# Rank matmuls behind a chunk's row products, and the first expert chosen after 12 chunks instead of 18

## The chip, the cores and the metric

The kernel runs on one core of a Trainium2 chip. Time is device microseconds (us) of one execution, and the figure for a kernel is the median of several runs. The engines are named as the profile names them: PE (TensorE), DVE (VectorE), ACT (ScalarE), POOL (GpSimd) and SP (SyncE, which here only issues DMAs). Each engine works through its own list of instructions in order and waits on semaphores for the others.

## What is computed

Three layers follow each other: a linear attention with a decaying state, a mixture of 8 experts in which each token goes to one expert, and a dense layer.

```
state = alpha[t] * state + k[t] (x) v[t];  y[t] = q[t] @ state       # 4 x 8 heads, 768 steps, 48 wide
x = y as 3072 rows of 384
e = argmax(x @ w_gate);  gate = softmax(x @ w_gate)[e];  eom = sigmoid(x @ w_output_gate)[e]
x = gate * eom * (relu(x @ w1[e]) @ w2[e])                           # 8 experts, 384 -> 1024 -> 384
out = relu(x @ w_in)**2 @ w_out                                      # 384 -> 2048 -> 384
```

## The kernel before

**Chunks.** Attention runs over 24 chunks of 128 tokens (six for each of four batch entries), all heads together, in the loop `for i in range(NCH - 2)`, with two chunks written out behind it. The program is in manual order: each engine executes what the Python code emits, in that order. Iteration i does several chunks' work at once: `scores(i + 1)` (key-query products, then the masked copies `m`, one by DVE and one by ACT and POOL's affine select), `scaled(i + 2)` (transposes of k and q into `tr`, scaled to `kh` and `qh` on DVE), `rows(i - 1)` and `logits(i - 1)` (chunk i - 1 turned to rows of tokens, the product `fx`, and the gate's logits), `decay(i + 3)` (transposes of alpha and two scans on DVE), `khat(i + 1)`, `outputs(i)` (the product `y`), `check(i)` and `update(i + 1)` (the product `u` and the state `st`). `load` refills a slot of k, q, alpha or v from SP's queue as soon as it is read; there are three or four slots of each.

**Routing.** Chunks are routed in groups of 6, 6, 6, 3, 1, 1 and 1. When a group's logits are there, `route` or `route_one` emits some small DVE steps, two at each `pulse()` between other work. `ranks` counts on PE where each token stands among its expert's tokens (`rk`), `place` and `placed` make of that a row index `idx` and a gate `g`, and `move` scales three tokens' chunks at a time (ACT for even, DVE for odd chunks) and scatters them with an indirect DMA on POOL to the table `xs`, which has a region for each expert. Before, `scores(i + 1)` emitted the rank matmuls ahead of its masks and `place` behind them: for the first two groups an iteration late (the set `waited`), for the later ones at once. Their result lay in the buffer of `y`, for three chunks in that of `ku`.

**The early start.** The experts' stage does not wait for all tokens. `pick` takes the expert with most tokens so far, `choose(0)` brings its number into an SP register (SP's queue waits for that), and `fetch` loads the raw float32 weights of six units of its hidden layer, two DMAs of 192 KB for each unit. `parts` splits a unit into two float32r parts: ACT copies, then DVE or POOL subtracts. `gather_early` reads the expert's first 256 rows from `xs`, `turn_early` transposes them (`tx`), and `up1(0)` is the first expert matmul (`ha`). Before, `pick` and the loads stood at the end of iteration 19 (NCH - 5) and took the counts of 18 chunks; of the first four units POOL subtracted two (iterations 20 and 22) and DVE two (both in iteration 21).

If the chosen expert has under 256 tokens (`few`), a general path runs behind the program; it is not taken for these inputs.

## Time and profile before

| | us |
|---|---|
| three runs | 831.48, 834.2, 836.35 |
| median | 834.2 |
| profiled execution, its own time | 830.97 |
| its span, first to last instruction | 829.2 |
| mean granted TensorE clock | 0.989 |

Of the span PE is busy 96%, DVE 60%, ACT 46% and POOL 28%; but the attention stage, up to about 169 us, has other limits than the rest: there DVE is busy 8 or 9 tenths of nearly every slice, and later 3 to 7. Times in the rows below are counted from the start of the span. The busy time of PE is modelled from the starts of its instructions, so a wait can hide in it; a wait stands in square brackets behind the row of the instruction that ended it.

### The profile page before, as it was taken

How to read it: one execution, taken by the hardware profiler on the slowest of the kernel's cores; microseconds unless marked ns; L12 is line 12 of the kernel's file. 1: busy time of each engine (PE TensorE's matmuls, PEld its weight loads, DVE VectorE, ACT ScalarE, POOL GpSimd, SP SyncE). 2: the span in 40 equal slices, each digit the busy share in tenths (PEclk: the TensorE clock that was granted, in tenths of full speed). 3: DMA queues.
4: the chain of work that ended last, by engine and by line, in shares of the span. 5: the costliest groups of instructions: out<-in, count | busy, mean ns of one | idle time of the engine just before them, and what ended most of it. 6: DMA issues, size and time to landing. Idle time of an engine off the chain costs nothing.

```text
span 829.2 us, 14100 instructions
## 1 busy us (share of the span) xinstructions
PE 796.7 (96%) x5215; PEld 731.1 (88%) x5215; DVE 498.4 (60%) x969; ACT 381.3 (46%) x734; POOL 228.6 (28%) x275
## 2 busy tenths in 40 slices
PE   7999999899999999999997999999999999999995
PEld 5899998798899999999986997999999999999995
DVE  8889999857355645876687787443333333333331
ACT  3677777554454555555444344332333333333221
POOL 3002341628456766777200000210002002002002
PEclk9999999899999999999998999999999999999998
DMA  9999994544554655674112110000000000000001
GB/s 135 179 210 180 209 175 99 185 132 157 156 161 128 182 149 152 167 181 127 39 58 76 58 58 21 39 13 27 0 1 39 1 1 38 1 1 39 1 0 42
DMA packets 153860, 74.98 MB, mean 90 GB/s; under 512 B 105406, under 2 KB 149430, under 8 KB 153782
## 3 DMA queue, kind: packets, MB, share of 16 engines
q1 hardware_dynamic: 149878, 64.52, 35.1%
q0 software_dynamic: 3904, 9.47, 3.1%
q8 instruction: 43, 0.70, 0.4%
q14 instruction: 35, 0.29, 0.1%
HBM read 61.76 MB, written 12.20 MB: 89 GB/s over the span
## 4 chain that ended last, share of the span: by engine, by line
PE 44%; issue 32%; DVE 14%; ACT 4%; POOL 3%; DMA 1%; SPq 1%; ACTq 0%; POOLq 0%; DVEq 0%
PE ha L1334 5%; PE ha L1336 5%; PE acc L1335 5%; PE acc L1334 5%; PE ha L1335 5%; PE acc L1336 5%; PE tr L268 3%; PE fx L425 2%; PE y L404 2%; POOL out_dram L129 2%; PE sc L337 2%; DVE r L929 2%; PE y L400 2%; ACT hh L933 2%; DVE bits L1346 1%
## 5 line engine op out<-in xcount | busy, mean ns | idle before, releaser
L1334 PE MATMUL ha<-xh,w 128*128 128x512 f32 (+7 forms) x456 | 173.9, 381 | 4.4 <-ACT xh L913 4.4
L1335 PE MATMUL ha<-xl,w 128*128 128x512 f32 (+7 forms) x456 | 172.3, 378 | 1.0 <-DVE xl L914 1.0
L1336 PE MATMUL ha<-xh,w 128*128 128x512 f32 (+7 forms) x456 | 172.5, 378 | 0.0
L929 DVE SCALAR_TENSOR_TENSOR r<-ha,r 128x512 f32<-128x512 f32 x96 | 66.3, 690 | 139.9 <-ACT r L928 137.6
L171 POOL TENSOR_TENSOR w<-raw,w 128x768 fp32r<-128x768 f32 x60 | 112.4, 1873 | 76.9 <-ACT w L170 73.9
L1334 PE MATMUL acc<-w,hh 128*128 128x384 f32 x384 | 130.6, 340 | 2.4 <-ACT half L946 1.8
L129 POOL DMA_INDIRECT out_dram<-o,ids x24 | 24.5, 1021 | 392.4 <-ACT o L954 359.8
L1336 PE MATMUL acc<-w,hl 128*128 128x384 f32 x384 | 130.6, 340 | 0.1
L1335 PE MATMUL acc<-w,hh 128*128 128x384 f32 x384 | 130.4, 340 | 0.0
L928 ACT ACTIVATE r<-ha 128x512 f32<-128x512 f32 x96 | 57.2, 596 | 144.4 <-PE ha L1336 144.3
L934 DVE TENSOR_TENSOR hl<-r,hh 128x512 fp32r<-128x512 f32 x96 | 66.6, 693 | 66.3 <-ACT hh L933 48.5
L1334 PEld LDWEIGHTS ha<-xh,w 128*128 128x128 f32 x456 | 85.9, 188 | 14.4 <-ACT xh L913 5.2
L1336 PEld LDWEIGHTS ha<-xh,w 128*128 128x128 f32 x456 | 85.8, 188 | 14.0
L933 ACT CAST hh<-r 128x512 fp32r<-128x512 f32 x96 | 59.5, 620 | 83.8 <-DVE r L929 82.6
L1335 PEld LDWEIGHTS ha<-xl,w 128*128 128x128 f32 x456 | 85.9, 188 | 11.6 <-DVE xl L914 1.9
L1334 PEld LDWEIGHTS acc<-w,hh 128*128 128x128 f32 x384 | 72.7, 189 | 7.3 <-ACT half L946 2.2
L170 ACT CAST w<-raw 128x768 fp32r<-128x768 f32 x64 | 53.5, 836 | 55.5 <-PE acc L1336 39.4
L1335 PEld LDWEIGHTS acc<-w,hh 128*128 128x128 f32 x384 | 72.7, 189 | 3.9
L1336 PEld LDWEIGHTS acc<-w,hl 128*128 128x128 f32 x384 | 72.7, 189 | 0.4 <-DVE hl L934 0.4
L703 DVE SCALAR_TENSOR_TENSOR hl<-ha,hh 128x448 fp32r<-128x448 f32 (+7 forms) x58 | 33.6, 580 | 54.8 <-ACT hh L700 52.3
L1334 PE MATMUL acc<-hh,w 128*128 128x448 f32 (+7 forms) x174 | 61.4, 353 | 0.0
L1335 PE MATMUL acc<-hl,w 128*128 128x448 f32 (+7 forms) x174 | 60.8, 350 | 0.1
(215 smaller groups left out, 1317.9 us busy)
## 6 DMA issues: line engine op xcount, KB each, us to landing
raw<-in_moe_w_dram SPq DMA_DIRECT2D x128, 192.0 KB
bits<-in_moe_w_in_dram SPq DMA_DIRECT2D x16, 384.0 KB
bits<-in_moe_w_out_dram SPq DMA_DIRECT2D x16, 384.0 KB
nat_al<-in_alpha_dram SPq DMA_DIRECT2D x24, 192.0 KB
nat_k<-in_k_dram SPq DMA_DIRECT2D x24, 192.0 KB
nat_q<-in_q_dram SPq DMA_DIRECT2D x24, 192.0 KB
nat_v<-in_v_dram SPq DMA_DIRECT2D x24, 192.0 KB
gx<-xs SPq DMA_DIRECT2D x22, 192.0 KB
```

What stands on the lines that cost most here:

```text
L129: ins = nc.gpsimd.indirect_dma_start(out=dst[:, :], out_offset=bass.IndirectOffsetOnAxis(ap=ix, axis=0), in_=src, in_offset=None)
L170: nc.scalar.copy(w[:, 0::2, :], raw)
L171: engine.tensor_tensor(out=w[:, 1::2, :], in0=raw, in1=w[:, 0::2, :].bitcast(F32), op=ALU.subtract)
L268: nc.tensor.transpose(ps[:, pr, :], src[:, pr, :], ident)
L703: nc.vector.scalar_tensor_tensor(out=hl, in0=ps, scalar=0.0, in1=hh.bitcast(F32), op0=ALU.max, op1=ALU.subtract)
L928: nc.scalar.activation(r, ps, AF.Relu)
L929: nc.vector.scalar_tensor_tensor(out=r, in0=ps, scalar=0.0, in1=r, op0=ALU.max, op1=ALU.mult)
L933: nc.scalar.copy(hh, r)
L934: nc.vector.tensor_tensor(out=hl, in0=r, in1=hh.bitcast(F32), op=ALU.subtract)
L1334: nc.tensor.matmul(ps, st[0], mv[0], start=start, stop=False)
L1335: nc.tensor.matmul(ps, st[0], mv[1], start=False, stop=False)
L1336: nc.tensor.matmul(ps, st[1], mv[0], start=False, stop=stop)
```

## The change

The rank matmuls and `place` leave `scores` and go to a new function `settle`, which is called behind `outputs(i)`, for each group as soon as it is routed. For a group of six their result lies in the buffer of `fx`. `pick` takes the counts of two groups (12 chunks) and stands in iteration 14, with `choose(0)` and the twelve loads; whether the chosen expert has 256 tokens after 18 chunks is asked by the new function `enough`, in iteration 20. `parts` of units 0 to 3 stand at the end of iterations 16, 17, 19 and 21, all with POOL's subtraction. Behind the loop, the last group's scaling and scatters (`send_group`) go from before `turn_early` to behind `outputs(23)`, and `turn_early` goes ahead of the logits of chunk 21.

```diff
@@ scores(i)
-            held = [(gi, ranks(gi)) for gi in list(routing) if gi in waited or gi >= PICK - 1]
-            waited.update(routing)
...
-            for gi, ps in held:
-                place(gi, ps)
+        def settle():
+            for gi in list(routing):
+                place(gi, ranks(gi))
@@ psum(n)
-                t = p_1.tile([P, BLK], F32, tag="ku" if n == 3 else "y", name="rk")
+                t = p_1.tile([P, BLK], F32, tag="fx" if n == GROUPS[0] else "y", name="rk")
@@ pick and enough
-            key = keys(PICK, ei8, "key0")
+            key = keys(PICK - 1, ei8, "key0")
-            nc.vector.tensor_scalar(few, mx, float(E * EARLY), None, op0=ALU.is_lt)
+        def enough():
+            n = keys(PICK, pre, "key1")
+            nc.vector.tensor_reduce(out=few, in_=n, axis=AX.X, op=ALU.max)
+            nc.vector.tensor_scalar(few, few, float((1 << 16) + E * EARLY), None, op0=ALU.is_lt)
@@ the loop
+        ready = [gstart[PICK - 1] + x for x in (4, 5, 7, 9)]
         for i in range(NCH - 2):
-            if i == NCH - 3:
-                parts(1, nc.vector)
...
-                parts(2, nc.vector)
...
             outputs(i)
+            settle()
...
-            if i == NCH - 5:
+            if i == gstart[PICK - 1] + 2:
                 pick()
                 for n in range(NRA + 2):
                     fetch(n)
             if i == NCH - 4:
+                enough()
                 gather_early()
-                parts(0)
+            if i in ready:
+                parts(ready.index(i))
@@ behind the loop, chunk 23
-        parts(3)
...
         i = NCH - 1
+        steps = [turn_early(kk) for kk in range(NK)]
+        settle()
         logits(i - 2)
         finish()
-        steps = [turn_early(kk) for kk in range(NK)]
         outputs(i)
+        send_group()
```

Three places where the order changes. On DVE, from the last product of chunk 23's `qh` to the one-hot of the group of three (iteration 21), before:

```order
L318 TENSOR_TENSOR qh<-tr,sp 128x512
L171 TENSOR_TENSOR w<-raw,w 128x2x384
L442 TENSOR_REDUCE lg<-fx 128x16
L171 TENSOR_TENSOR w<-raw,w 128x2x384
L463 TENSOR_REDUCE mx<-lg 128x3
L466 TENSOR_TENSOR df<-lg,mx 128x24
L471 SCALAR_TENSOR_TENSOR cand<-df,em_94 128x24
```

and after:

```order
L318 TENSOR_TENSOR qh<-tr,sp 128x512
L442 TENSOR_REDUCE lg<-fx 128x16
L463 TENSOR_REDUCE mx<-lg 128x3
L466 TENSOR_TENSOR df<-lg,mx 128x24
L471 SCALAR_TENSOR_TENSOR cand<-df,em_94 128x24
```

The two weight subtractions `w` have left DVE's list. On POOL, from iteration 19 to the split in iteration 21 of the changed kernel (`xs` is the scatter of a chunk, `m` the mask of a chunk's second half of heads; five more pairs of memset and scatter stand where the dots are):

```order
L171 TENSOR_TENSOR w<-raw,w 128x2x384
L347 AFFINE_SELECT m<-m 128x512
L128 MEMSET apart 128x1
L129 DMA xs<-xn,idx 24576x384
...
L347 AFFINE_SELECT m<-m 128x512
L171 TENSOR_TENSOR w<-raw,w 128x2x384
```

Before, the six scatters of chunks 12 to 17 stood three and three, with a mask between them; now all six stand in a row ahead of the mask of chunk 22, and a split stands ahead of them and another behind that mask. On SP, at the end of iteration 14 of the changed kernel, the choice and the first of twelve weight loads:

```order
L260 DMA nat_al_156<-in_alpha_dram 128x8x48
L260 DMA nat_v_174<-in_v_dram 128x8x48
L148 TENSOR_LOAD first
L148 ISA x2
L159 ISA
L159 DMA raw<-in_moe_w_dram 128x3x128
L160 ISA
L160 DMA raw<-in_moe_w_dram 128x384
```

Behind the twelfth stand the loads of k, q, alpha and v for iterations 15 and on, 16 in all; before, the choice stood behind the loads of iteration 19, which are the last of them.

## Rows read from the trace of the kernel before

**Rows 1.** Busy time by stretch: us, then busy us (instructions) of each engine, granted clock, DMA
```profile
107.60:113.84 6.24, 6.24 (x84) 5.94 (x81) 5.47 (x12) 4.84 (x12) 1.66 (x3) 1.00 0.91 147
...
145.54:153.27 7.73, 6.61 (x80) 5.84 (x76) 6.57 (x10) 5.90 (x11) 6.72 (x9) 1.00 0.95 305
153.27:157.31 4.04, 1.17 (x20) 1.07 (x17) 3.83 (x13) 0.77 (x3) 1.55 (x2) 0.80 0.52 190
```
**Rows 2.** The same view in stretches of 2 us, around the half clock
```profile
154.00:156.00 2.00, 0.43 (x8) 0.34 (x7) 1.93 (x6) 0.03 (x1) 0.82 (x1) 0.93 0.62 232
156.00:158.00 2.00, 0.69 (x7) 0.68 (x7) 1.86 (x9) 0.92 (x3) 0.00 (x0) 0.50 0.04 16
...
160.00:162.00 2.00, 2.00 (x14) 1.77 (x15) 1.04 (x1) 0.92 (x2) 1.10 (x1) 0.50 0.00 0
162.00:164.00 2.00, 2.00 (x23) 1.83 (x20) 1.96 (x7) 0.58 (x1) 1.07 (x3) 0.86 0.00 0
```
**Rows 3.** PE in order of time: start, us, line, instruction [idle before, what ended it]
```profile
126.66 0.66 PE L268 MATMUL tr<-ident,nat_k 128*128 128x128 f32 x4
...
157.31 0.18 PE L503 MATMUL rk<-onehot,tri 128*128 128x24 bf16 x1 [2.88 <-DVE st L385]
...
162.82 0.87 PE L692 MATMUL tx<-ident,gx 128*128 128x128 f32 x6
163.53 1.06 PE L400 MATMUL y<-qh,both 128*128 128x128 f32 x8
...
169.29 0.39 PE L1334 MATMUL ha<-early,w 128*128 128x256 f32 x1
```
**Rows 4.** DVE in order of time, same columns, iterations 19 to 21
```profile
140.94 0.16 DVE L653 SCALAR_TENSOR_TENSOR key<-cps,ei 128x8 f32<-128x8 f32 x1
...
144.02 1.22 DVE L294 TENSOR_TENSOR_SCAN sp<-al,ends 128x512 f32<-128x512 f32 x1
...
149.98 0.68 DVE L318 TENSOR_TENSOR qh<-tr,sp 128x512 f32<-128x512 f32 x1
151.78 2.54 DVE L171 TENSOR_TENSOR w<-raw,w 128x768 fp32r<-128x768 f32 x1 [1.12 <-issue]
...
154.38 1.25 DVE L171 TENSOR_TENSOR w<-raw,w 128x768 fp32r<-128x768 f32 x1
...
156.40 0.18 DVE L479 SCALAR_TENSOR_TENSOR onehot<-ei,em 128x24 bf16<-128x24 f32 x1
```
**Rows 5.** ACT in order of time, iteration 20: the scaling of a chunk
```profile
144.40 0.66 ACT L574 ACTIVATE xn<-xn,g 128x384 f32<-128x384 f32 x1
```
**Rows 6.** POOL in order of time: scatters of group 2 and the last of all
```profile
148.15 0.97 POOL L129 DMA_INDIRECT xs<-xn,idx  x1 [0.59 <-DVE xn L572]
...
150.69 0.96 POOL L129 DMA_INDIRECT xs<-xn,idx  x1 [0.19 <-issue]
...
174.19 0.96 POOL L129 DMA_INDIRECT xs<-xn,idx  x1 [0.19 <-ACT early L700]
```
**Rows 7.** SP in order of time: first weight load, early gather, last gather of the first expert
```profile
142.71 0.40 SPq L159 DMA_DIRECT2D raw<-in_moe_w_dram  x1
...
157.24 0.89 SPq L684 DMA_DIRECT2D gx<-xs  x2
176.93 0.86 SPq L892 DMA_DIRECT2D rest<-xs  x2
```
**Rows 8.** PE in order of time: a wait in the first chunks
```profile
25.27 0.66 PE L268 MATMUL tr<-ident,nat_al 128*128 128x128 f32 x4 [1.63 <-DMA nat_al<-in_alpha_dram]
```
**Rows 9.** Busy time by stretch, around that wait
```profile
24.00:26.00 2.00, 0.73 (x7) 0.73 (x8) 0.85 (x3) 0.60 (x2) 0.63 (x1) 1.00 1.50 166
```
**Rows 10.** Groups by line, 200 to 400 us: POOL's splits, busy us, mean ns | idle before
```profile
L171 POOL TENSOR_TENSOR w<-raw,w 128x768 fp32r<-128x768 f32 x55 | 103.2, 1877 | 64.9 <-ACT w L170 61.9 <-DMA gx<-xs 1.0 <-DMA raw<-in_moe_w_dram 0.9
```
**Rows 11.** The same view of DVE, 200 to 400 us: a step beside the splits
```profile
L1346 DVE SCALAR_TENSOR_TENSOR bits<-sq,bits 128x384 f32<-128x384 f32 x16 | 21.6, 1350 | 16.0 <-ACT sq L1344 14.2 <-DMA gx<-xs 1.9
```
**Rows 12.** The same view, 400 to 600 us: the same DVE step without POOL's splits
```profile
L1346 DVE SCALAR_TENSOR_TENSOR bits<-sq,bits 128x384 f32<-128x384 f32 x16 | 8.9, 556 | 0.5
```

More of the change, by code (lines that the diff above doesn't have):

```diff
@@ L446, in logits @@
                 agenda.append((route if GROUPS[gi] > 1 else route_one)(gi))
-        routing, waited = {}, set()
+        routing = {}
         def route(gi):
@@ L638, in place_one, with send_group @@
                                            scalar=float(E * NT), in1=ix, op0=ALU.add, op1=ALU.add)
+        def send_group():
+            for i, g in moving:
+                x = xn.pop(i)
+                nc.vector.tensor_scalar(x, x, g, None, op0=ALU.mult)
+                scatter("xs", xs, idx[:, i:i + 1], x)
         def send(i):
@@ L802, in moe_block_kernel @@
         rows(i - 1)
-        parts(3)
         finish()
         outputs(i)
-        for i, g in moving:
-            x = xn.pop(i)
-            nc.vector.tensor_scalar(x, x, g, None, op0=ALU.mult)
-            scatter("xs", xs, idx[:, i:i + 1], x)
         i = NCH - 1
+        steps = [turn_early(kk) for kk in range(NK)]
+        settle()
         logits(i - 2)
         finish()
-        steps = [turn_early(kk) for kk in range(NK)]
         outputs(i)
+        send_group()
         one = group[i - 2][0]
```

## The prediction

> **What bounds the kernel now.** I read the busy times by stretch first, to find where attention stops running at its normal pace, then the engines in order of time inside that place, and last the DMA issues. A normal chunk takes 6.24 us, and PE is busy in all of it [rows 1]: in the middle of attention PE sets the pace, and work that DVE, ACT or POOL do beside it is free while they keep up. That ends near iteration 21. The stretch from 145.54 is 7.73 us long with 6.61 us of PE work, and the next is 4.04 us long with 1.17 us of PE work [rows 1]. The reader is to see who held it: DVE's `qh` ends at 150.66, then DVE waits 1.12 us and subtracts a weight for 2.54 us, takes the logits, and subtracts another for 1.25 us; only then come the one-hot at 156.40 and the state, for which the rank matmuls waited 2.88 us [rows 3, 4]. PE had so little to do that its granted clock fell to half: 0.93 on average in 154 to 156, 0.50 from 156 on, 0.86 in 162 to 164 [rows 2]. From the averages the half clock lasted 0.28 + 6 + 0.56 = 6.8 us. The first expert matmul starts at 169.29 [rows 3]. From there PE is the bound almost to the end (busy 96% of the span), so what that start gains should reach the end of the kernel; it is the quantity that I forecast.
>
> **DVE's halves go.** Two weight subtractions leave DVE, and with them the wait for ACT's copies: from the end of `qh` to the one-hot were 156.40 - 150.66 = 5.74 us, of which 1.12 + 2.54 + 1.25 = 4.91 us [rows 4] fall away. On its own this puts the one-hot at 151.5. The rank matmuls now stand ahead of `u` and the scores of chunk 23 (1.17 us busy [rows 1], and I estimate 0.6 for `u`). The products from 157.31 to 162.82 took 5.51 us, nearly all at half clock; at full clock I take 2.9. So chunk 22's products end at about 151.5 + 0.2 + 0.6 + 1.2 + 2.9 = 156.4, instead of 162.82: over 6 us earlier.
>
> **But the early gather then ends last.** The transposes `tx` stand next on PE, and they need the 256 gathered rows. Before, these were long there. The gather waits for the scatters of chunks 12 to 17, and the change makes those later: their group is placed behind `outputs(19)`, not ahead of it, so its reciprocal comes right behind the scan of iteration 20, and all six scatters follow in a row. The scan started at 144.02 [rows 4]. Three things move it. The choice leaves iteration 19: seven small steps of about 0.16 us, -1.05 us. In iteration 14 these steps come between PE's count and the next `fx`, in whose buffer the count lies: I take +0.5 us, bounds 0 and 1.05. POOL's splits delay DVE: +0.25 us, below. I take the scan at 143.7. It lasts 1.22, the reciprocal 0.2, ACT's scaling 0.66 [rows 5]: first scatter at 145.8. Three scatters started from 148.15 to 150.69, one each 1.27 us [rows 6]. So the sixth starts at 152.15 and ends on POOL at 153.1; before it ended at 151.65. What gains here is the rest of the way. The old gather was issued at 157.24, 5.6 us behind the last scatter, because twelve weight loads had been sent from 142.71 on [rows 7]; the last gather of this expert, with no such load in the queue, followed its scatter's end (174.19 + 0.96) by 1.78 us [rows 6, 7]. That gives an issue at 154.9. The old one moved nothing any more from 160.00 on [rows 2], so it needed at most 2.76 us: rows there at 157.7. With `tx` (163.53 - 162.82 = 0.71 us [rows 3]) chunk 23's `y` starts at 158.4 instead of 163.53. **Gain: 5.1 us.** PE waits about 1.3 us ahead of `tx`; a wait of 1.63 us left the clock at 1.00 [rows 8, 9], one of 2.88 us did not [rows 2, 3]. So I expect no half clock. From that `y` to the first expert matmul were 5.76 us [rows 3], in a chain of PE, ACT and DVE steps that stays. The three scalings of the last group move behind `outputs(23)`, but the DVE steps for which they wait are done while PE runs that product. I leave it at 5.76.
>
> **What must stay hidden.** Four ACT copies move to iterations 16, 17, 19 and 21; in a normal chunk ACT is busy 4.84 of 6.24 us [rows 1], so each has room, and two scalings leave iterations 16 and 17. If the cover fails, the copy (the same work as before, then in iterations 20 to 22) delays the scan behind it by its own length, under 1 us. On POOL a split of 1.88 us [rows 10] fits into a chunk where POOL is busy 1.66 [rows 1], behind the mask of one chunk and ahead of the next. What it does to DVE is the open cost: the step L1346 takes 1.350 us where splits run and 0.556 where none does [rows 11, 12], +0.8 us for a step that is hit. Three splits come before the scan of iteration 20: bounds 0 and 2.4 us. I take 0.25, since DVE has 0.8 us to spare in a normal chunk (5.47 of 6.24 [rows 1]) and only the third split meets a full one.
> The rule that speaks against the change is in the Trainium skill, SBUF — State Buffer, section "Who interferes with whom": a VectorE instruction with two SBUF inputs and a GpSimd instruction that reads SBUF share a port, and who comes second waits for the whole instruction of the first. The trace agrees in kind (2.54 us for a subtraction beside POOL's, 1.25 without), but its mean price is half a split or less. By the rule each split could stop a scan for its full 1.88 us, 5.6 us for three, and nothing would be left of the gain.
>
> The moved choice holds SP's queue in iteration 14 until DVE has it, by estimate near 111 us (the next chunk's PE work starts at 107.60 [rows 1], DVE ends its share some 2 us behind PE, and the seven steps take 1.05), and then twelve loads of 192 KB; before, the first went out 0.1 us behind the choice's last steps and the data of all twelve had come by about 156, 13 us later (0.62 DMA share in 154 to 156, 0.04 after [rows 2, 7]). So the loads of chunk 20's k, q, alpha and v wait until 111 + 13 = 124; k is needed at 126.66 [rows 3]. Its own load needs 1 to 2 us more. It fits with about 1 us left; bounds of this cost: 0, and 3 us if k comes at 129.
>
> For the default inputs the counts, taken from the reference, give the same first expert after 12 chunks (215 tokens) and after 18 (319, above 256), so neither the general path nor another order of experts comes in.
>
> **Rivals.** (1) The gather comes 1.2 us later or more, by splits, copies or slower scatters, and PE waits long enough to fall to half clock as before. Then `tx`, `y` and two `fx`, some 4.5 us at full clock, take up to 3.4 us more (6.8 at half [rows 2]): gain 5.1 - 1.2 - 3.4 = 0.5, **833.7**. For it: six scatters in a row; against it: a wait of 1.63 us did no harm. (2) The splits stop DVE's scans for their full length: three times 1.88 us [rows 10], 5.6 us, in place of my 0.25: gain 5.1 + 0.25 - 5.6 = -0.2, **834.4**; against it stands +0.8 in rows 11 and 12. (3) Slower than before: the loads of k, q and alpha for chunk 20 come behind the weights and PE stands still in iteration 18. With k late by d us the loss is d, and from about 2.7 us on also 3.4 us for the half clock. At d = 5, k at 131.7, the gain turns into 5.1 - 5 - 3.4 = -3.3, **837.5**; it decides from d = 1.7 if the clock falls with it. For it: only about 1 us of slack; against it: the queue is idle at 111, and has three scatters beside it, not six as at 142. (4) The chain behind `y` also shortens, because its ACT and DVE steps are no longer late behind POOL and half-clock products: of its 5.76 us perhaps 2.5, gain 7.6, **826.6**.
>
> **How the numbers follow.** Forecast 0.52, rival 1 0.18, rival 2 0.10, rival 3 0.09, rival 4 0.11. The sum stands against the profiled execution: 830.97 - 5.1 = 825.9. The median of the three runs is 834.2, 3.2 above, so I forecast 829.1. The forecast's own spread is about 2.5 us on either side (scan 143.0 to 145.5, loads 0 to 1 late). The range from 824.5 to 835.0 leaves out rival 3, and the ends of rival 4. A difference of 0.5%, 4.2 us, is about what a measurement of this kernel can tell from no change: faster by more, 0.53 (most of the forecast, rival 4); within, 0.38; slower by more, 0.09.
>
> **What would show it.** In the changed profile: no DVE weight subtraction before the first expert matmul; that matmul at about 164.2; PE's longest wait ahead of `tx`, released by the gather, under 2 us, and the granted clock at 1.00 from 140 to 170; the six scatters from about 146 to 153 and the gather's issue near 155. Wrong would be: PE waiting for nat_k or nat_al near 127 (rival 3), DVE scans of 2 us and more beside splits (rival 2), a clock of 0.5 near 158 (rival 1). If the start of the experts comes earlier as forecast and the time does not, a later stage has taken the gain back.

## The result

The changed kernel takes 839.6 us (median of 8 runs, 835.3 to 841.04) against 832.5 for the kernel before on the same chip: ratio 1.0072, 95% interval 1.0048 to 1.0096. It is 7 us slower, by 0.7%; I had forecast 829.1 and a gain of 5.1. The profiled execution took 839.43 us, its span is 837.6 (before 829.2), the mean granted clock 0.985 (before 0.989).

To see where the time went, I followed one marker through both traces: the start of each chunk's scores on PE, then the first expert matmul, then the issue of the rest gather (of the first expert's other rows) on SP. The other columns are runs described below.

```
us from the span's start      before   after  e1_clear  e2_enough  e3_rank_fx  e4_send  e5_all  e12_late_question
scores of chunk 12             82.43   83.42     83.12      82.00       82.50    82.26   82.71     81.95
scores of chunk 13             89.49   93.67     90.56      88.91       91.86    93.03   89.13     88.19
scores of chunk 20            130.96  137.60    133.64     132.01      136.58   139.13  132.20    130.39
scores of chunk 22            145.54  151.47    147.50     145.76      150.43   152.98  145.94    144.14
scores of chunk 23            153.27  163.63    159.59     157.58      159.46   165.52  154.03    152.25
first expert matmul           169.29  175.78    171.82     168.86      169.94   177.69  168.15    163.36
rest gather issued            176.93  185.32    181.06     178.03      179.15   185.24  175.71    170.92
end of the span               829.2   837.6     833.5      833.3       831.9    837.9   831.7     823.9
```

After against before: +1.0 at chunk 12, +4.2 at chunk 13, +6.6 at chunk 20, +5.9 at chunk 22, +10.4 at chunk 23, +6.5 at the first expert matmul, +8.4 at the rest gather and at the end (8.4 us between the two profiled executions, 7.1 between the medians). So there are three places of loss and a slow one between them, and nothing changes behind 185 us.

**First place, chunks 11 to 13.** SP of the changed kernel in order of time (start, us, line, instruction, and in brackets the wait before it), then POOL, then PE:

```profile
73.40 1.15 SPq L260 DMA_DIRECT2D nat_v<-in_v_dram  x1
...
80.56 0.58 SPq L684 DMA_DIRECT2D xs<-zero  x1
```
```profile
77.24 1.12 POOL L129 DMA_INDIRECT xs<-xn,idx  x1 [0.19 <-issue]
...
78.36 1.51 POOL L347 TENSOR_SCALAR_AFFINE_SELECT m<-m 128x512 f32<-128x512 f32 x1
...
84.78 1.90 POOL L129 DMA_INDIRECT xs<-xn,idx  x1 [4.87 <-DVE d L302]
...
89.80 2.09 POOL L347 TENSOR_SCALAR_AFFINE_SELECT m<-m 128x512 f32<-128x512 f32 x2
```
```profile
88.18 0.43 PE L404 MATMUL y<-m,nat_v 128*64 128x128 f32 x2
...
91.35 1.35 PE L404 MATMUL y<-m,nat_v 128*64 128x128 f32 x13 [2.74 <-POOL m L347]
```

SP stands still from 74.55 to 80.56 ahead of the last of the eight zero fills of `xs`: the fill must not overtake the scatters that were emitted before it, and since groups are now placed an iteration earlier, three scatters stand ahead of it instead of one. POOL's fourth scatter in turn starts only at 84.78, and behind the sixth stand two masks at once; PE has begun chunk 11's product and waits 2.74 us for its mask. The clock goes with it (busy us of each engine, then granted clock):

```profile
90.00:92.00 2.00, 0.65 (x10) 0.65 (x12) 1.32 (x2) 0.00 (x0) 1.89 (x2) 0.95 1.17 310
92.00:94.00 2.00, 2.00 (x26) 1.91 (x24) 0.22 (x1) 0.99 (x2) 0.00 (x0) 0.50 1.24 209
```

**Second place, chunk 22 to 23.** DVE's two subtractions are gone, as the change says, and the one-hot follows `qh` by 1.0 us, not by 5.7 as in [rows 4]. But DVE, PE, ACT and POOL now read:

```profile
155.37 0.16 DVE L659 SCALAR_TENSOR_TENSOR key<-cps,pre 128x8 f32<-128x8 f32 x1
...
158.72 0.18 DVE L479 SCALAR_TENSOR_TENSOR onehot<-ei,em 128x24 bf16<-128x24 f32 x1
```
```profile
155.67 1.12 PE L425 MATMUL fx<-wx,yt 128*128 128x112 f32 x8 [2.02 <-ACT xn L574]
...
162.83 0.17 PE L503 MATMUL rk<-onehot,tri 128*128 128x24 bf16 x1 [2.09 <-ACT yt L409]
...
170.83 0.88 PE L703 MATMUL tx<-ident,gx 128*128 128x128 f32 x6
```
```profile
162.19 0.59 ACT L409 COPY yt<-y 128x512 f32<-128x512 f32 x1 [3.64 <-PE y L404]
```
```profile
153.29 1.29 POOL L129 DMA_INDIRECT xs<-xn,idx  x1 [2.05 <-ACT xn L574]
...
159.95 0.96 POOL L129 DMA_INDIRECT xs<-xn,idx  x1 [0.19 <-issue]
```

`fx` waits 2.02 us for the key of `enough`, whose count lies in its buffer. (The bracket names ACT's scaling, which ended at the same moment as the key; e2 and e6 below show that it is the key.) The rank matmuls, now in the buffer of `y`, could run at 158.9 but wait for ACT's copy of that product; and the copy starts 1.3 us after the last of six scatters and 1.46 us after the product's own end (159.26 + 1.47). The clock falls to 0.67 in 156 to 158 and is 0.50 from 164 to 170. The transposes `tx` stand at 170.83 instead of 162.82 [rows 3], though the gather, issued at 162.56, needs about 2.5 us (e12 below): its rows were there near 165.

**Third place, behind the first expert matmul.** The distance to the rest gather grows from 7.64 to 9.54 us. ACT of the changed kernel, and POOL:

```profile
179.85 0.38 ACT L711 ACTIVATE early<-ha 128x256 fp32r<-128x256 f32 x1 [2.12 <-PE ha L1345]
```
```profile
177.89 0.96 POOL L129 DMA_INDIRECT xs<-xn,idx  x1 [0.19 <-DVE ix L617]
```

The first `relu` of the experts waits 2.12 us though its matmuls had ended; it writes a buffer of the ring in which the token rows `xn` lay, and the last group's scatters, which read those rows, now go out from 174.07 on.

### The profile page after: what moved, and what is told of

It is laid out like the page before. It is cut to its first block, busy times and chain, and to the rows that moved or that the text cites. A ratio compares the mean times of both kernels' runs of the same rounds, so it can differ in the third digit from the quotient of the medians.

```text
span 837.6 us, 14115 instructions
## 1 busy us (share of the span) xinstructions
PE 802.6 (96%) x5216; PEld 735.7 (88%) x5216; DVE 498.3 (59%) x969; ACT 380.9 (45%) x734; POOL 233.3 (28%) x277
## 4 chain that ended last, share of the span: by engine, by line
PE 46%; issue 32%; DVE 11%; ACT 6%; POOL 3%; DMA 1%; SPq 0%; ACTq 0%; POOLq 0%; DVEq 0%
PE ha L1343 5%; PE ha L1345 5%; PE acc L1343 5%; PE ha L1344 5%; PE acc L1344 5%; PE acc L1345 5%; PE tr L268 3%; PE sc L337 3%; PE y L404 3%; POOL out_dram L129 2%; PE fx L425 2%; DVE r L938 2%; PE y L400 2%; ACT hh L942 2%; DVE hl L943 1%
## 5 line engine op out<-in xcount | busy, mean ns | idle before, releaser
L171 POOL TENSOR_TENSOR w<-raw,w 128x768 fp32r<-128x768 f32 x62 | 116.0, 1871 | 92.5 <-ACT w L170 90.2
```

Source lines behind the costliest of these rows:

```text
L171: engine.tensor_tensor(out=w[:, 1::2, :], in0=raw, in1=w[:, 0::2, :].bitcast(F32), op=ALU.subtract)
```

## Experiments

Every kernel was timed beside the kernel before on its chip; ratios are to that.

**The zero fill (e1_clear).**

```diff
-            if 1 <= i <= E:
+            if 1 <= i < E:
                 clear(i - 1)
+            if i == E - 1:
+                clear(i)
```

> The changed kernel with one thing moved: the last of the eight zero fills of the table goes out in iteration 7, ahead of all scatters, instead of at the end of iteration 8, behind three scatters of group 0. Theory (three separate stumbles, this is the first): the fill waits on SP for the third scatter (from 74.55 to 80.56 us), the fourth scatter on POOL waits for the fill, the mask of chunk 11 stands behind the scatters, and PE's product of chunk 11 waits 2.74 us for that mask and drops to half clock. Without it the scores of chunk 13 start near 89.7 instead of 93.67, the clock stays at 1.00 there, and the time falls by 4 us (3 to 5), to about 835.5. Rival: six scatters packed into two iterations delay the masks by themselves, or the loads of k and q are late whatever the fill does; then the scores of chunk 13 stay after 92.5 and the gain is under 1.2 us, 838.4 or more.

Ratio 1.0017 (0.9996 to 1.0038), span 833.5. POOL's mask and fourth scatter now read

```profile
79.60 0.65 POOL L347 TENSOR_SCALAR_AFFINE_SELECT m<-m 128x512 f32<-128x512 f32 x1
...
80.46 0.97 POOL L129 DMA_INDIRECT xs<-xn,idx  x1 [0.16 <-issue]
```

with a wait of 0.16 us in place of 4.87, the scores of chunk 13 follow those of chunk 12 by 7.44 us (10.25 after, 7.06 before), and the clock is 1.00 from 84 to 94. The theory held: with one DMA moved ahead in SP's queue, the span is 4.1 us shorter. The other runs bear it out: from the scores of chunk 12 to those of chunk 14, five of the six profiled kernels with the ranks moved and the fill in its old place (after, e3, e4, e6, e11) took 16.3 to 19.2 us, and the seven with the fill moved ahead too (e1, e5, e8, e9, e10, e12, e13) 11.7 to 12.8. The sixth, e2_enough, took 12.3: the chain was as late (4.2 us from fill to fourth scatter, as in the changed kernel), but the next three scatters took POOL 3.5 us instead of 5.0, and PE waited only 0.24. So how much it costs varies.

**The question and the buffer (e2_enough, e3_rank_fx).** Two edits of what I took for one loss.

```diff
@@ e2_enough: enough() leaves iteration 20
-                enough()
                 gather_early()
...
+        enough()
         key = keys(len(GROUPS), pre, "key")
@@ e3_rank_fx: psum(n)
-                t = p_1.tile([P, BLK], F32, tag="fx" if n == GROUPS[0] else "y", name="rk")
+                t = p_1.tile([P, BLK], F32, tag="fx" if n > 1 else "y", name="rk")
```

> The changed kernel with the question whether the first expert has 256 tokens (function enough: a count on PE in fx's buffer and three DVE steps) moved from the end of iteration 20 to where all counts are read, after the first expert's start. Theory: its key, late on DVE behind three scalings and the state, is what holds fx of chunk 20 by 2.02 us; the wait takes the clock to half, and that makes the product of chunk 21 and the rank matmuls behind it late. Without it fx starts within 0.3 us of the transposes' end, the clock stays at 1.00, the scores of chunk 23 start 4 us earlier (8.2 us behind those of chunk 22 instead of 12.2), and the time falls by 3.5 to 5 us, to about 835.3. From there the early gather, behind six scatters, ends last, with a PE wait ahead of tx of 1 to 2 us. Rival: the rank matmuls, now in the buffer of y, wait for the copy of y anyway, and PE falls to half clock there; then the gain is under 1.5 us, 838 or more.

> The changed kernel with the rank matmuls of the group of three in the buffer of fx, not of y, so that they need not wait for ACT's copy of chunk 21's product; nothing else differs, the order is the same on every engine. Theory (fx's wait for the count of enough is the cause, the buffer a part of its consequence): fx of chunk 20 still waits 2 us and the clock still falls; the rank matmuls follow the product at once, which gives back 0.7 us, bounds 0.3 and 1.5: 838.9. Rival (the buffer is the cause): the rank matmuls start at about 159, as soon as the one-hot is there, and the gain is 2.5 to 4 us, 836 to 837.

e2_enough: ratio 1.0105 (1.0067 to 1.0142). `fx` waits 0.5 us, but from scores to scores chunk 23 still takes 11.82 us: the rank matmuls wait 4.29 us for the copy, which itself starts 3.65 us after its product; the product had run at full clock, and the clock falls to 0.50 only behind the wait (156 to 160). (The profiled execution of e2 was the fastest of its four, 835.03 us against a median of 838.14, so its span in the table flatters it.) e3_rank_fx: ratio 1.0029 (1.0010 to 1.0048), 9.03 us for that step. My theory fell and the rival stood: the buffer is the larger part, the question a small one. One thing is mixed into the figure: `fx` waited 2.03 us here too, and the clock stayed at 1.00, where in the changed kernel it fell, so from one profile the buffer's share and the clock's can't be parted. And at the place where it was put, behind the first expert matmul, the question costs more than in the old one: from that matmul to the end 664.4 us in e2_enough, 661.8 in the changed kernel.

**The last group's scatters (e4_send).**

```diff
         i = NCH - 1
+        send_group()
         steps = [turn_early(kk) for kk in range(NK)]
...
         outputs(i)
-        send_group()
```

> The changed kernel with the last group's three scalings and scatters back ahead of the transposes tx, where they stood before the change. Theory: the first relu of the experts (ACT, 179.85, 2.1 us idle) writes into a buffer that the scattered rows of this group still occupy, so it waits until the last of the three late scatters has landed. With the scatters ahead again the relu comes within 0.5 us of its matmuls, the distance from the first expert matmul to the rest gather falls from 9.54 to about 7.6 us, and the time by 1.9 us (1.2 to 2.3), to 837.6. Rival: the three scalings on DVE push the steps ahead of the first expert matmul back by their own 1.1 us and eat the gain: first expert matmul 0.7 us or more later, time within 0.6 us of the changed kernel.

The step from first expert matmul to rest gather is 7.55 us again, as before, and the `relu` follows with no wait:

```profile
179.63 0.38 ACT L711 ACTIVATE early<-ha 128x256 fp32r<-128x256 f32 x1
```

In time it does not show: ratio 1.0069 (1.0046 to 1.0092), and this execution lost 2.8 us more than the changed kernel's between chunks 12 and 14. The mechanism is shown, its worth in the whole is not.

**All four (e5_all).** The four diffs in one.

> The four edits in one: zero fill ahead of the scatters, question enough after the first expert's start, rank matmuls of the group of three in the buffer of fx, last group's scatters ahead of tx. Theory (three separate losses that add): from the changed kernel's profiled 839.4 us the fill gives 4.1 back, the buffer and the question together 5, the scatters 2: about 828.5 (826.5 to 830.5), faster than the kernel before by 0.3 to 0.7%; the scores of chunk 23 start 8 to 8.5 us behind those of chunk 22. Rival: the early gather, issued only after six scatters in a row, is the next to end last, and PE waits for it ahead of tx; then the first expert matmul is no earlier than 167 and the time 830.5 to 832.5, the same as the kernel before.

Ratio 0.9999 (0.9981 to 1.0017): the 7 us are back, the forecast gain is not. The theory (828.5) fell; the time is near the rival's, but `tx` does not wait for the gather. The question behind the first expert matmul takes some 3 us of it (663.6 us from there to the end; e4_send 660.2). The rest is in chunk 23, and its rows show what I had not thought of. PE, POOL, ACT and DVE of e5_all:

```profile
151.18 1.09 PE L404 MATMUL y<-m,nat_v 128*64 128x128 f32 x16
...
155.10 0.47 PE L337 MATMUL sc<-qh,kh 48*128 48x128 f32 x2 [0.36 <-issue]
...
155.79 0.36 PE L337 MATMUL sc<-qh,kh 48*128 48x128 f32 x1 [0.22 <-issue]
...
156.51 0.57 PE L337 MATMUL sc<-qh,kh 48*128 48x128 f32 x5 [0.35 <-issue]
```
```profile
147.88 1.30 POOL L129 DMA_INDIRECT xs<-xn,idx  x1 [2.04 <-ACT xn L574]
...
154.54 0.96 POOL L129 DMA_INDIRECT xs<-xn,idx  x1 [0.19 <-issue]
```
```profile
156.55 0.59 ACT L409 COPY yt<-y 128x512 f32<-128x512 f32 x1 [3.75 <-remote]
```
```profile
156.55 0.18 DVE L526 TENSOR_TENSOR rp<-rk,onehot 128x24 f32<-128x24 f32 x1 [2.96 <-remote]
```

The product of chunk 21 ends at 152.27. ACT's copy of it and DVE's product with the rank matmuls (run at 153.24) both start at 156.55, "remote", and PE stops three times within the scores without a wait of its own. All of it ends about 1 us behind the last of six scatters on POOL. In after, e1, e3, e4, e5, e9 and e2 the copy starts 1.0 to 1.3 us (e2: 0.4) after the sixth scatter's end, whatever the product's end: 1.4 us behind it in after, e1 and e4, 2.9 in e3, 3.7 in e2, 4.3 here and in e9. Below, a row of scatters with nothing but their memsets between them is called a train, and a signal is late when ACT or DVE stands idle although the PE result that it needs has ended in the profile.

**Three and three (e6_place2, e8_all_place2).** The third group's rank matmuls go back ahead of the masks of chunk 20, in `y`'s buffer, so that a mask parts its scatters; once on the changed kernel, once on all four edits.

```diff
@@ scores(i), behind the matmuls, and behind the masks
+            held = [(gi, ranks(gi, "y")) for gi in list(routing) if gi == PICK - 1]
...
+            for gi, ps in held:
+                place(gi, ps)
```

> The changed kernel with only the rank matmuls of the third group of six put back ahead of the masks of chunk 20, in the buffer of y, so that its scatters come three, a mask, three again. Theory (a train of six scatters on POOL delays what PE reports to ACT and DVE: the copy of chunk 21's product came 1.2 to 1.5 us after the product and 1.2 us after the last scatter in four kernels, whatever the product's own end): with two trains of three the copy follows the product within 0.3 us, the scores of chunk 23 start 9 to 10.5 us behind those of chunk 22 instead of 12.2, the gather goes out 2 us earlier; gain 2 to 4 us, 835.5 to 837.5. Rival: the copy is late for another reason in chunk 21's own work; then it stays over 1 us behind the product and the gain is under 1 us.

> The four edits together and, on top, the third group of six placed ahead of the masks of chunk 20 as in the kernel before, so that its scatters come three and three and end about 2 us earlier. Theory (train of six delays signals and the gather): 1 to 2.5 us faster than the four edits alone, about 826.5, PE's wait ahead of tx under 0.5 us. Rival (the gather and the train are covered once the other waits are gone): within 0.7 us of the four edits alone.

In e6 the copy of chunk 21's product starts at 164.60, 0.1 us behind it; but the last scatter had ended at 162.01, 2.5 us before the product, so this tells little about trains. Nothing is gained: 1.0072 (1.0045 to 1.0098), and e8 is slower than e5: 1.0042 (1.0021 to 1.0063). Two things cost.

Ahead of the masks the rank matmuls wait for the one-hot (1.94 us in e6, 1.95 in e8), and chunk 21 starts 8.4 us behind chunk 20 in e6, where the clock stayed at 1.00, and 10.1 us in e8, where it fell to 0.50 in 136 to 138; in after and e5 it is 6.8. So placing a group behind `outputs` is worth 1.6 to 3.2 us there: the part of the change that does what it should.

And one of DVE's scans met the whole of a split. DVE and POOL of e8:

```profile
149.44 3.46 DVE L303 TENSOR_TENSOR_SCAN sp<-al,d 128x512 f32<-128x512 f32 x1
```
```profile
149.97 1.84 POOL L171 TENSOR_TENSOR w<-raw,w 128x768 fp32r<-128x768 f32 x1
```

The scan takes 3.46 us, where it takes 1.23 otherwise, and ends 1.1 us behind the split. PE then waits 2.12 us for the state in e8, and in e6, with a scan of 3.45 us, `fx` waits 3.44 us for the key instead of 2.02. So these two runs are no clean test of three and three.

**Each half of the change alone (e7_early_only, e11_settle_only).**

```diff
@@ e7_early_only, on the kernel before; the question stands at the end
-            key = keys(PICK, ei8, "key0")
+            key = keys(PICK - 1, ei8, "key0")
...
-            if i == NCH - 5:
+            if i == gstart[PICK - 1] + 2:
                 pick()
...
+            if i in ready:
+                parts(ready.index(i))
@@ e11_settle_only, on the kernel before
             outputs(i)
+            settle()
```

> The kernel before with only the early choice of the first expert (12 chunks, iteration 14), its twelve weight loads there, and the four splits by GpSimd in iterations 16, 17, 19 and 21; the question enough stands after the first expert's start; rank matmuls, scatters and tx stay where they were. Theory (the forecast's core: the two halves on DVE and the weight loads ahead of the gather were what held the end of attention): the one-hot of the group of three comes 3 to 5 us earlier, the half clock near 158 is shorter or gone, the first expert matmul 2.5 to 5 us earlier, ratio to the kernel before 0.994 to 0.997. Rival: what the splits and the loads cost in chunks 16 to 21 (0.4 us for each scan that meets a split) and scatters behind splits eat it: ratio 0.999 or more.

> The kernel before with only the other half of the change: the rank matmuls behind a chunk's product, as soon as a group is routed, in the buffers of the change (fx for six chunks, y for three); choice, loads and splits stay where they were, the question enough and the moves of tx and scatters are not in it. Theory: the stall at the last zero fill comes with it whole (scores of chunk 13 start over 9 us behind those of chunk 12, half clock), the wait of 1.9 us for the one-hot in chunk 20 goes, and the six scatters in a row delay what follows; ratio 1.003 to 1.007. Rival: these stalls come only together with the early choice; then the ratio is 0.997 to 1.001.

e7: 1.0005 (0.9983 to 1.0028), no gain. DVE and PE in iteration 19:

```profile
130.53 1.59 DVE L294 TENSOR_TENSOR_SCAN sp<-al,ends 128x512 f32<-128x512 f32 x1 [0.26 <-ACT al L288]
```
```profile
134.80 0.22 PE L503 MATMUL rk<-onehot,tri 128*128 128x48 bf16 x1 [1.94 <-DVE onehot L479]
```

This scan meets the end of a split and takes 1.59 us (two others took 2.23 and 3.46, and behind the longest PE waited 2.13 us for the state). PE waits 1.94 us for the one-hot and its transposes run at half speed behind it (1.09 us for four, 0.66 in [rows 3]); chunk 21 starts 10.9 us behind chunk 20. The first expert matmul still comes 1.3 us earlier than before, and 1.68 us of waiting for another one-hot follow. e11: 1.0068 (1.0029 to 1.0106), as slow as the whole change: chunk 13 starts 10.1 us behind chunk 12, and at chunk 21 the rank matmuls wait 6.9 us for ACT's copy, since DVE's halves are still there and ACT stands behind them. So the rearranged ranks alone lose as much as the whole change, though at chunk 21 by another route; the early choice alone is about even.

**Breaking the train (e9_best, e10_split).** e9 is e5 with the question in iteration 19. e10 moves, on top, the second three scatters and the early gather into iteration 21, behind the scores, so that the mask of chunk 22 stands between them.

```diff
@@ e10_split, the loop
             scores(i + 1)
+            if i == NCH - 3:
+                move(pace)
+                gather_early()
...
             outputs(i)
-            move(pace)
+            if i != NCH - 4:
+                move(pace)
             update(i + 1)
-            move(pace)
+            if i != NCH - 4:
+                move(pace)
```

> As the four edits together, but with the question enough at the end of iteration 19, where its count is ready and no scaling stands ahead of its key on DVE, instead of after the first expert's start. Theory: behind the first expert matmul the question cost 1.7 us of PE's time (its second count waits for the key of the first) and delayed what follows (from the first expert matmul to the end 663.6 us, against 660.2 where the question stayed and only the scatters were moved); in iteration 19 it costs at most 0.3 us. So the stretch behind the first expert matmul is 660 to 660.5 us again, and the time is 2.5 to 3.3 us below the four edits, about 829.7, ratio to the kernel before 0.996 to 0.998. Rival: the wait of fx for the key comes back in chunk 19 with the half clock; then the first expert matmul is 2 us later and the time is that of the four edits.

> The kernel with the question in iteration 19 and the three other edits, and on top the six scatters of the third group of six broken by the mask of chunk 22: three in iteration 20, three and the early gather in iteration 21 behind the scores; the rank matmuls stay behind the product of chunk 19. Theory (signals of PE come late while a train of more than three scatters runs): ACT's copy of chunk 21's product and DVE's product with the rank matmuls follow PE within 0.5 us instead of 2.9 to 4.3, no stops of PE inside the scores of chunk 23, clock 1.00 there; chunk 22's product ends 2.5 to 3.5 us earlier than with six in a row. The gather goes out 0.7 to 1 us later, so PE then waits for it ahead of tx, 1.5 to 2.5 us; the first expert matmul gains 0 to 1.5 us. Rival: the lateness comes from the product's own place or from the gather's descriptors, not from the train; then the copy stays 3 us late and the first expert matmul comes 1 us later with the gather.

e9: 0.9997 (0.9977 to 1.0017). Behind the first expert matmul 660.7 us, near the 660 to 660.5 of the theory, but the count now waits in the same buffer for the rank product (view of waits: what waited, for what, us in total, times, longest):

```profile
PE cps L657 <- DVE rp L526: 1.7, 1, 1.7
```

e10: 0.9978 (0.9956 to 1.0000). ACT, DVE, PE, and the stretch ahead of `tx`:

```profile
153.16 0.57 ACT L409 COPY yt<-y 128x512 f32<-128x512 f32 x1
```
```profile
154.11 0.18 DVE L526 TENSOR_TENSOR rp<-rk,onehot 128x24 f32<-128x24 f32 x1
157.41 0.36 DVE L385 TENSOR_TENSOR st<-u,st 128x192 f32<-128x192 f32 x1 [3.13 <-PE fx L425]
```
```profile
151.91 1.09 PE L404 MATMUL y<-m,nat_v 128*64 128x128 f32 x16
...
160.62 0.33 PE L703 MATMUL tx<-ident,gx 128*128 128x128 f32 x1 [1.52 <-DMA gx<-xs]
```
```profile
156.00:158.00 2.00, 1.84 (x15) 1.54 (x14) 0.56 (x4) 0.00 (x0) 0.53 (x1) 1.00 0.43 160
```

The copy follows the product (ends at 153.00) by 0.16 us and DVE follows the rank matmuls by 0.1; no stop inside the scores, and the clock is 1.00 throughout. For these two signals the theory held. But the lateness has moved and is not gone: the state `st` starts 2.8 us behind the end of `u` (154.58), 0.9 us behind the third scatter of the second train (156.53). Behind the first expert matmul ACT and DVE take the results of `fx` 1.6 and 2.1 us late, behind a train of four (162.98 to 167.76), and the step to the rest gather is 9.76 us, against 7.56 in e9. So a train need not be six long. The early gather did not hold the signals, since in e5 it went out at 157.15, behind the late copy. In e10 it is the next to end last, as forecast: PE waits 1.52 us for it.

**The question out of the way, and the splits (e12_late_question, e13_no_subtract).** e12 is e10 with `enough` called in `judge`, with a PSUM tile of its own; e13 is e12 with POOL's subtraction replaced.

```diff
@@ e12_late_question
-            if i == NCH - 5:
-                enough()
...
         def judge():
+            enough()
@@ e13_no_subtract, parts(n) for n < NRA
-            engine.tensor_tensor(out=w[:, 1::2, :], in0=raw, in1=w[:, 0::2, :].bitcast(F32),
-                                 op=ALU.subtract)
+            nc.gpsimd.memset(w[:, 1::2, :].bitcast(F32), 0.0)
```

> The kernel with the broken train of scatters, and the question enough asked only where the kernel decides on the general path, in the dense layer, with a PSUM buffer of its own. Theory (in iteration 19 its count waited 1.7 us for DVE's product with the rank matmuls, which lie in the same buffer; the scores of chunk 21 came 8.7 us behind those of chunk 20): that distance falls to about 6.9 us, PE's wait for the count is gone, and the first expert matmul comes 1 to 1.8 us earlier; time 1 to 1.8 us below the broken train with the question in iteration 19, ratio to the kernel before 0.995 to 0.997. Rival: DVE, not the count, holds chunk 20, and PE then waits that long for the gather ahead of tx: first expert matmul within 0.5 us of 166.4, ratio 0.997 to 0.999.

> As the kernel with the late question, but GpSimd does not subtract for the first four units: it only fills their low halves with zeros, so the first expert's first four hidden units are multiplied without the low part of their weights (this part of the computation is left out). The loads, ACT's copies and the choice stay. Theory A (the splits beside DVE's scans are what lengthens chunks 13 to 20, 43.1 us from scores to scores against 41.5 in the kernel before): the scans in chunks 17 to 20 take 1.22 us again instead of 1.5 to 1.6, and those chunks together 1 to 1.6 us less. Theory B (the early choice in iteration 14 and ACT's four copies cost it, not the splits): scans shorter but the stretch from chunk 13 to 20 within 0.5 us of the kernel with splits.

e12: 825.23 against 827.91 us, ratio 0.9970 (0.9961 to 0.9979): 0.3% faster than the kernel before. e13: 0.9969 (0.9959 to 0.9979), the same. PE and a stretch of e12, then DVE of e12 and of e13 in the same chunk:

```profile
158.45 1.21 PE L706 MATMUL tx<-ident,gx 128*128 128x128 f32 x6 [2.03 <-DMA gx<-xs]
...
163.36 0.36 PE L1351 MATMUL ha<-early,w 128*128 128x256 f32 x1
```
```profile
156.00:158.00 2.00, 0.42 (x8) 0.18 (x4) 1.96 (x6) 0.59 (x1) 1.71 (x3) 1.00 0.48 131
```
```profile
129.22 1.60 DVE L294 TENSOR_TENSOR_SCAN sp<-al,ends 128x512 f32<-128x512 f32 x1 [0.26 <-ACT al L288]
```
```profile
129.08 1.23 DVE L299 TENSOR_TENSOR_SCAN sp<-al,ends 128x512 f32<-128x512 f32 x1 [0.27 <-ACT al L293]
```

The edit does what its theory says: the wait of 1.7 us for the count is gone, and chunk 21 follows chunk 20 by 6.85 us (8.69 in e10). But e12 differs from e10 in more. Up to the end of iteration 19 the two are the same program; rows of POOL and ACT of e10, then of e12, at the same place in iteration 17:

```profile
119.13 0.96 POOL L129 DMA_INDIRECT xs<-xn,idx  x1 [0.19 <-issue]
```
```profile
121.13 0.59 ACT L409 COPY yt<-y 128x512 f32<-128x512 f32 x1 [1.80 <-PE y L404]
```
```profile
117.94 0.96 POOL L129 DMA_INDIRECT xs<-xn,idx  x1 [0.19 <-DVE qh L318]
```
```profile
118.86 0.59 ACT L409 COPY yt<-y 128x512 f32<-128x512 f32 x1 [0.72 <-PE y L404]
```

The product ended at 119.96 in e10 and at 118.75 in e12, so the copy came 1.2 us late in one and 0.1 in the other, each time beside the third scatter of a train. In e12 and e13 no step of ACT or DVE in attention starts more than 0.75 us behind the PE result that it waited for; in every other profiled run, that of the kernel before included, some step beside or just behind a train of three starts 1.0 us late or more. e12 and e13 ran on another chip than e1 to e11. So of the 3.1 us by which the first expert matmul of e12 comes before that of e10 (166.43; expected were 1 to 1.8), the question's part cannot be told from that of the late signals. The two ratios, each to the kernel before on the same chip, lie within each other's noise.

Without the subtractions the scans are 1.22 to 1.23 us long again; still, chunks 13 to 20 take 42.13 us in e13 and 42.20 in e12, against 41.47 before and 43.93 in the changed kernel. Theory B's number stands for that stretch: 0.7 us are left without splits, and they lie before the first split (chunks 13 to 17: 25.15 us in both, 24.35 before). Its cause stands in part. The step from chunk 16 to 17, in which DVE makes the choice, is 0.45 us longer (6.69 us, 6.24 before). But the step from 14 to 15, ahead of the choice, is 0.33 us longer (6.65, 6.32 before), and it is so in e11, which has no early choice, and not in e7, which has nothing else: that part belongs to the moved ranks. From chunk 20 to 23 the splits do cost 1.4 us (21.86 against 20.46), which does not reach the end of the kernel.

## Why the prediction failed, step by step

The chain that I forecast is close to that of e12, and far from that of the changed kernel:

```
                              forecast   after   e12_late_question
one-hot of the group of three   151.5   158.72   151.23
first of six scatters           145.8   153.29   146.07
chunk 22's products end         156.4   170.90   156.41
early gather issued             154.9   162.56   155.92
transposes tx                   157.7   170.83   158.45
product of chunk 23             158.4   171.54   159.50
first expert matmul             164.2   175.78   163.36
```

Part of the closeness is luck. In e12 the product of chunk 23 starts 1.1 us later than forecast and the rest is 1.9 us shorter, and the two nearly cancel; its scatters stand three and three, not six in a row as I had reckoned; and no late signals came in.

- **DVE's halves go.** Right in kind: the wait and the subtractions left, and the one-hot follows `qh` at once. What replaced them I had not seen.
- **The early gather ends last.** Wrong for the changed kernel, where `tx` waited for PE's own late work; right once that was cleared (1.52 us in e10, 2.03 in e12). The terms held: issue 1.65 us after the last scatter (forecast 1.8), rows there 2.5 us later (at most 2.76).
- **"Group placed behind outputs", counted only for its scatters' time.** This is the first step that failed. I priced the later start of the third group and took the earlier start of the first two at nothing, without reading what stood behind their scatters: a zero fill on SP, and through it POOL's next scatter and a mask. That place was worth 4.1 us in e1.
- **Buffers, not costed.** This is the second step that failed, and where most was lost: from the scores of chunk 22 to those of chunk 23 the changed kernel takes 12.2 us, 7.7 before. The rank matmuls went from `ku` to `y`, where they need ACT's copy; the prediction's 0.2 us for them holds only where nothing reads the buffer. With e3 this and the clock were 3.1 us of chunk 23.
- **Six in a row, counted as 1.27 us each.** Their time on POOL was right. That ACT and DVE get PE's results late beside a train was in no term; rival 1 sought "slower scatters" in the gather only. It could have been read before: in the kernel before, the third scatter of a train and the copy of a product that had ended at 145.15, 1.6 us earlier, read

```profile
144.97 1.04 POOL L129 DMA_INDIRECT xs<-xn,idx  x1 [0.19 <-issue]
```
```profile
146.78 0.59 ACT L409 COPY yt<-y 128x512 f32<-128x512 f32 x1 [1.72 <-PE u L378]
```

- **`send_group` at nothing.** The third step that failed, by 1.9 us: the steps that it waits for are indeed done in time, but I looked at what it waits for and not at who waits for the buffers it reads.
- **The choice.** +0.5 us (0 to 1.05): 0.45 in the step from chunk 16 to 17 of e12, as forecast (0.16 in e7, where the ranks stand as before).
- **The splits.** +0.25 us for DVE, bounds 0 and 2.4: in the changed kernel the two scans that met a split (at 129.94 and 136.43) took 0.4 us more each, so rival 2 did not come there; but in e6, e7 and e8 one scan each took 2.2 us more. The price was misread: it is not a share of the split, but what is left of it when DVE's step begins. The scan of e12 above began at 129.22, beside a split from 127.92 to 129.74: 0.52 us were left, and it took 0.38 us more. In [rows 4] DVE's half began with 1.72 us of a POOL split left (151.68 to 153.50) and took 2.54 us, where 0.96 is its time beside none (e12, at 168.96). In all 29 scans and subtractions of DVE up to 200 us that met a split, in the profiles of before, after and e1 to e12, the added time is what was left of the split, less 0.13 to 0.16 us. The rule of the Trainium skill, SBUF — State Buffer, section "Who interferes with whom", has the later one wait for the whole instruction of the first; the trace agrees, in size too (1.60 us against 1.23 in the same scan of e12 and e13, 3.46 in e8, where the scan began beside the scatter that the split followed at once).
- **Rival 3** did not come: k of chunk 20 was there when PE reached it. (In the kernel before the first weight load went out 0.63 us behind the last of the choice's steps, which ended at 142.08; the prediction's 0.1 is misread, but nothing hangs on it.)
- **Tail of 5.76 us.** Shorter: 4.24 in the changed kernel, 3.86 in e12, as rival 4 had it.

So the chain that I forecast for the end of attention does come about once other losses are cleared, and the loss lies where I had costed moves at nothing. In the profiles the three are worth 4.1 us (e1, whole span), 4.8 (e3, from the scores of chunk 22 to the first expert matmul) and 2.0 (e4, from there to the rest gather), but the executions differ by some us of their own, and only e1, e3 and the combined kernels show it in time.

Two things stay open. The first is why 5.9 us at the first expert matmul of e12 are only 2.5 us in its ratio. The 5.9 are taken from a profile of the kernel before on another chip, in an execution of 830.97 us; on e12's chip its median is 827.91, 3.1 us less, and that is about the difference. What makes it shorter there is not shown, as there is no profile of it from that chip; late signals that do not come there would fit. The second is by what way late signals go with a train of scatters, and why they do not in e12 and e13. That the scatters cause them is argued from where the lateness ends, and is not shown; and as the ends of matmuls are modelled, it may be PE that ends late and not its signal.

## What to carry to other kernels

When a group of DMAs is issued earlier, read what is queued behind it on every queue that must not overtake it: a zero fill on another engine's queue cost 4.1 us here, of a forecast gain of 5.1. When a result moves to another buffer, list who reads and who refills that buffer, and price the wait for the slowest of them; a move that needs nothing itself can still be waited for. When work moves to POOL, look which of DVE's steps begin beside it, and how much of it is then left. And when several such costs stand in series, build the version that has none of them before giving up the idea: here it was worth 0.3%. Compare it with the old kernel on the same chip only.

## What the runs showed of the hardware that was not expected

- Behind trains of indirect scatters from POOL (one each 1.27 us), ACT and DVE took up results of PE late: with six in a row 1.4 to 4.3 us late, 0.4 to 1.3 us behind the last scatter's end, and in e3, e5 and e9 PE itself stopped between matmuls without a wait; with three, 1.6 us in the kernel before (the copy at 146.78) and 2.8 in e10 (the state at 157.41). In e12 and e13, on another chip, the same trains of three went with none of it, though e12 is the same program as e10 up to the end of iteration 19.
- A scan or subtraction of DVE that began while POOL subtracted took longer by what was left of POOL's instruction, less 0.13 to 0.16 us, in 29 cases of 29: from 0.2 us (e12, 1.44 us at 122.89) to 2.2 us (e8, 3.46 us).
- A wait of 2.03 us in e12 and one of 2.03 in e3 left PE's granted clock at 1.00; 2.02 us at the same instruction as in e3 were followed by 0.67 and then 0.50 in the changed kernel. The same wait for a one-hot, 1.94 us in e6 and 1.95 in e8, left 1.00 in the one and was followed by 0.50 in the other. The length of a single wait does not tell which it will be, so the prediction's two cases (1.63 us harmless, 2.88 not) made no rule.
